# Issuing most of the V-cache transfers of a decode-attention kernel from ScalarE's queue

## The chip, the cores and the metric

The kernel runs on one core of one Trainium2 chip. The metric is the device time of one execution in microseconds (us); before the change it is 369.37 us, the median of three runs (369.34 to 369.59).

The core has five instruction streams that matter here: TensorE (PE, matrix products), VectorE (DVE), ScalarE (ACT), GpSimd (POOL) and SyncE (SP). A stream runs its instructions in order; a wait at the head of a stream holds everything behind it. Two of the streams, SP and ACT, issue the transfers between HBM and the on-chip memory in this kernel. The transfers themselves are carried by 16 DMA engines, which all streams share.

## The reference

One decode step with eight sequences (B = 8, one new token each, D = 576). Branch A is attention over the last W = 2048 positions of a cache; branch B is a small MLP; a gate per sequence mixes them.

```python
x = A_x; g = sigmoid((x * gate_w).sum(-1, keepdims=True))
# A: 32 query heads, 16 KV heads, Dh = 128, the last W = 2048 of 8192 positions
q = (x @ wq)                                  # per head 128 wide
k = repeat(k_cache[:, :, Sk - W:, :], 2)      # two query heads share a KV head
v = repeat(v_cache[:, :, Sk - W:, :], 2)
p = softmax(einsum("bhqd,bhkd->bhqk", q, k) * Dh ** -0.5)
a = einsum("bhqk,bhkd->bhqd", p, v) -> (B, 1, 32 * 128) @ wo
# B
b = gelu(layernorm(x) @ w1 + b1) @ w2 + b2
out = g * a + (1 - g) * b
```

All of it is bf16 in HBM. K and V in the window are 8 x 16 x 2048 x 128 elements each, 64 MiB each; the weights wq, wo, w1 and w2 add some 20 MB. The profile counts 154.31 MB read.

## The kernel before, in words

**Units.** K and V are each cut into 32 units of 2048 KB. A unit holds four sequences of one KV head, laid out as 128 rows of 16 KB, one row to a partition. Four units in a row (two KV heads, all eight sequences) form a group g; there are eight groups, and a softmax is done for each group at once.

**Slots.** The units, and the weights wo and w2, go through a ring of nine slots of on-chip memory (`NSLOT = 9`). Slots are handed out in the order of one list, `stream` (lines 549 to 560): K0 to K4, then K5, V0, K6, V1, K7, V2 and so on alternately, with a chunk of wo (W0 to W3, 1152 KB each, rows of 1152 bytes) after V7, V15, V23 and V31, then the bias b2 and four chunks of w2 (M0 to M3). The thing that takes a slot has to wait until the ninth thing before it in that list has been used up: a K unit's slot is free once VectorE has transposed it (`tr`, line 642, two per unit), a V unit's slot once TensorE has multiplied with it (`pv`, line 682).

**A K unit** (`k_unit`, line 624): its transfer (`dk`, line 627); two transposes on VectorE (line 642); two times eight matmuls of scores on TensorE (lines 659 and 173; `qk`). After the fourth K unit of a group comes the softmax (line 584): a maximum (`mx`, line 587), small operations, four exponentials on ScalarE (`exp`, line 601) and four transposes of the result on VectorE (line 606).

**A V unit** (`v_unit`, line 671): its transfer (`dv`, line 675), 16 matmuls (`pv`, line 682), a copy out of PSUM on ScalarE (`uev`, line 691, two buffers), four small matmuls (`us`, line 697), and for every second unit another small copy on ScalarE (`oev`, line 707) and a multiplication.

**The order.** No order is written out by hand. `_Plan.schedule` (line 62) lays out all operations with estimated costs: at each step it takes the ready operation with the earliest estimated start, each engine one after the other, all large transfers one after the other at an estimated bandwidth. Each engine then gets its operations in that order (`emit`, line 141) with waits on semaphores: one semaphore per engine, one per slot for the transfers (`"s%d" % s`). A V transfer is also kept behind the transfer before it in `stream` in the plan's time (`after=last_dma[-1:]`), which orders but adds no wait.

**Queues.** All 32 K, all 32 V, and all weight transfers are issued by SP, in the order of `stream`. ACT issues four small loads at the start (x, gate_w twice, b1) and one of the two output stores. PSUM and all compute stay as they are in the change.

Of the kernel before, what the change touches and what calls it, by code (L numbers as in the profile page):

```python
# [38 lines left out]
class _Plan:  # L39
# [10 lines left out]
    def add(self, eng, fn, deps=(), name=None, cost=0.1, after=(), prio=0):  # L50
        op = _Op(eng, fn, deps, name, cost, after=after, prio=prio)
        op.idx = len(self.all)
        self.all.append(op)
        return op

    def dma(self, eng, fn, semkey, nbytes, deps=(), name=None, after=(), prio=0):
        op = _Op(eng, fn, deps, name, self.DMA_ISSUE, after=after, is_dma=True, dma_sem=semkey, nbytes=nbytes, prio=prio)
        op.idx = len(self.all)
        self.all.append(op)
        return op  # L60
# [119 lines left out]
def build_kernel(nc, A_x, A_k_cache, A_v_cache, A_wq, A_wo, B_x, B_w1, B_b1, B_w2, B_b2, gate_w, out):  # L180
    B, Sq, D = A_x.shape
    _, Hkv, Sk, Dh = A_k_cache.shape
    Hq = A_wq.shape[1] // Dh
    F = B_w1.shape[1]
    W = min(4096, max(256, Sk // 4))
# [6 lines left out]
    NSLOT = 9  # L192
# [12 lines left out]
    with ExitStack() as es:  # L205
# [119 lines left out]
        def slot(s):  # L325
            return RAW[:, s * SE:(s + 1) * SE]
# [18 lines left out]
        OC = 64  # L345

        eng_sems = {e: es.enter_context(nc.semaphore("sem_" + e)) for e in ENGS}
        dma_keys = ["x", "b", "b2", "wq", "w1", "out", "outb"] + ["s%d" % i for i in range(NSLOT)] + ["t%d" % i for i in range(4)]
        dma_sems = {k: es.enter_context(nc.semaphore("dma_" + k)) for k in dma_keys}

        P = _Plan()
        add, dma = P.add, P.dma
# [39 lines left out]
        for s in range(2):  # L392
            o_xz.append(add("dve", (lambda s=s: lambda e: e.tensor_copy(xz[:, s, :].rearrange("p (k z) -> p k z", z=2)[:, :, s], x_sb[:, 512:576]))(),  # L393
                            deps=dx + [o_xz0], name="xz%d" % s, cost=0.12))
# [12 lines left out]
        for s in range(2):  # L407
            o_yz.append(add("dve", (lambda s=s: lambda e: e.tensor_copy(yz[:, s, :].rearrange("p (k z) -> p k z", z=2)[:, :, s], y_bf[:, 512:576]))(),
                            deps=[o_y, o_yz0], name="yz%d" % s, cost=0.12))
# [30 lines left out]
        def b1ev_fn(e):  # L440
# [5 lines left out]
                   deps=[o_dga, o_dgb, o_onesf], name="g_pe", cost=0.4, after=[o_yTp])  # L446
# [7 lines left out]
        for q in range(4):  # L454
            o_i32.append(add("dve", (lambda q=q: lambda e: e.tensor_copy(i32[32 * q:32 * q + 32, :], ident[32 * q:32 * q + 32, 32 * q:32 * q + 32]))(),
                             deps=[o_ident, o_obl], name="i32_%d" % q, cost=0.15, prio=-1))
# [91 lines left out]
        NUQ = 4 * NG  # L548
# [13 lines left out]
        last_dma = [d_w1r]  # L562
        slot_free = [[o_qp]] * 3 + [[o_hp]] * 3 + [[]] * 3
# [11 lines left out]
        def src_of(cache, g, q):  # L575
            hkv, b0 = 2 * g + q // 2, 4 * (q % 2)
            return cache[b0:b0 + 4, hkv, S0:Sk, :].rearrange("a (x r) d -> x a (r d)", x=32)

        def take_slot():
            n = n_slot[0]  # L580
            n_slot[0] += 1
            return (n + 6) % NSLOT
# [88 lines left out]
        def v_unit(i):  # L671
            g, q = divmod(i, 4)
            s = take_slot()
            item = 2 * g + q // 2
            d = dma("sp", lambda e: e.dma_start(slot(s), src_of(A_v_cache, g, q)), "s%d" % s, 4 * W * Dh * 2, deps=slot_free[s], name="dv%d" % i, after=last_dma[-1:])  # L675
            last_dma.append(d)

            def pv_fn(e):
                mm = None
                for t in range(16):  # L680
                    c = 32 * (t % 4)
                    mm = e.matmul(ps[c:c + 32, BK_OS[i % 2], :], PT[:, g % 2, 512 * q + 32 * t:512 * q + 32 * t + 32], slot(s)[:, 512 * t:512 * t + 512],  # L682
                                  start=(t < 4), stop=(t >= 12), skip_group_check=True, tile_position=(0, c))
                return mm
            deps = [d] + pt_done[g] + ([u_ev[i - 2]] if i >= 2 else [o_qT, o_u])
            prev = add("pe", pv_fn, deps=deps, name="pv%d" % i, cost=1.5, after=pv_hist[-1:])
            pv_hist.append(prev)
            slot_free[s] = [prev]
            if q == 3:
                pv_last[g] = prev  # L690
            u_ev[i] = add("act", lambda e: e.activation(out=EV[:, i % 2, :], in_=ps[:, BK_OS[i % 2], :], func=ACTF.Copy),  # L691
                          deps=[prev] + ([u_sum[i - 2]] if i >= 2 else []), name="uev%d" % i, cost=0.8, prio=3)

            def us_fn(e):
                mm = None
                for r in range(4):
                    mm = e.matmul(ps[:, BK_S, OC + 16 * (item % 2) + 8 * (q % 2):OC + 16 * (item % 2) + 8 * (q % 2) + 8], EV[:, i % 2, 128 * r:128 * r + 128], i32[:, 8 * r:8 * r + 8],  # L697
                                  start=(r == 0), stop=(r == 3), skip_group_check=True)
                return mm
            u_sum[i] = add("pe", us_fn, deps=[u_ev[i]] + o_i32 + b6_r[-2:], after=b6_w[-1:], name="us%d" % i, cost=1.0, prio=3)  # L700
            b6_w.append(u_sum[i])
            if q % 2 == 1:
                hl = q // 2
                prev = u_sum[i]
                osrc = ps[:, BK_S, OC + 16 * (item % 2):OC + 16 * (item % 2) + 16]
                if item < Hkv - 1:
                    ev = add("act", lambda e: e.activation(out=o32[:, item % 2, :], in_=osrc, func=ACTF.Copy), deps=[prev] + ([oT_done[item - 2]] if item >= 2 else []), name="oev%d" % item, cost=0.25, prio=3)  # L707
                    o_item_ev[item] = ev
                    b6_r.append(ev)
                    eng, src_, deps = "pool", o32[:, item % 2, :], [ev, rg_done[g]]  # L710
                else:
                    eng, src_, deps = "dve", osrc, [prev, rg_done[g]]

                def om_fn(e):
                    return e.tensor_tensor(out=oT[:, item, :, :].rearrange("p h b -> p b h"), in0=src_.rearrange("p (b h) -> p b h", h=2),  # L715
                                           in1=rg[:, g % 2, 16 * hl:16 * hl + 16].rearrange("p (b h) -> p b h", h=2), op=ALU.mult)
                oT_done[item] = add(eng, om_fn, deps=deps, name="oT%d" % item, cost=0.25, prio=9)
# [37 lines left out]
        for kind, i in stream:  # L755
            {"K": k_unit, "V": v_unit, "W": wo_chunk, "M": m2_chunk, "B": bias}[kind](i)
# [37 lines left out]
def bass_gated_mix__sliding_block_cached__mixer_channel_mlp__decode_kernel(  # L794
    nc: bass.Bass,
    A_x: bass.AP,
    A_k_cache: bass.AP,
    A_v_cache: bass.AP,
    A_wq: bass.AP,
    A_wo: bass.AP,  # L800
    B_x: bass.AP,
    B_w1: bass.AP,
    B_b1: bass.AP,
    B_w2: bass.AP,
    B_b2: bass.AP,
    gate_w: bass.AP,
    out: bass.AP,
):
    build_kernel(nc, A_x, A_k_cache, A_v_cache, A_wq, A_wo, B_x, B_w1, B_b1, B_w2, B_b2, gate_w, out)
# [28 lines left out]
```

## Time and profile before

| What | Value |
|---|---|
| median of three runs | 369.37 us |
| span of the profiled execution, first to last instruction | 367.9 us |
| its own whole time | not given apart from its span; the median lies 1.5 us above the span |
| TensorE busy | 263.5 us (72%), mean granted clock 0.852 of full |
| VectorE busy | 210.4 us (57%) |
| ScalarE busy | 47.8 us (13%) |
| queue of SP (q1) | 154.29 MB, its packets took 98.9% of the 16 DMA engines' span |
| queue of ACT (q10) | 56 packets, 0.03 MB |
| a V transfer, from issue to landing | 34.1 us median, 16.2 to 39.8 |
| a K transfer, from issue to landing | 33.3 us median, 20.1 to 40.5 |

How to read it: the time of a stream is "busy" only while it computes; waiting and issuing transfers don't count. The row of queues says how much of the time of all 16 DMA engines the packets of one queue filled. "From issue to landing" is the time a transfer spends waiting in its queue behind earlier ones and being carried; where it is many times what the carrying takes, there is a queue of transfers in front of it.

### The profile page before, as it was taken

Reading aid. Unit: us, or ns where it says so; the run is one execution under the profiler, and the core shown is the slowest. Engines: PE = TensorE matmul, PEld = TensorE weight load, DVE = VectorE, ACT = ScalarE, POOL = GpSimd, SP = SyncE. Lnnn points to the kernel's source line nnn. Section 1 sums busy time; section 2 is a strip of 40 time slices with the busy share of each in tenths; the row PEclk is TensorE's granted clock in tenths of the full one; section 3 lists DMA queues with packets and bytes.
Section 4 is the critical chain, followed back from the end, with each engine's and each line's share of the span. In section 5 each row is a group of like instructions: output and inputs, shape, how many; then the busy total and the mean of one; then the engine's idle time right before and its main releaser. Section 6 shows DMA issues by size and latency. Waiting matters only on the chain.

```text
span 367.9 us, 4129 instructions
## 1 busy us (share of the span) xinstructions
PE 263.5 (72%) x1837; PEld 87.0 (24%) x1429; DVE 210.4 (57%) x253; ACT 47.8 (13%) x117; POOL 37.5 (10%) x163
## 2 busy tenths in 40 slices
PE   0349984797698589773986399774976398773984
PEld 0339200122132022110321032110321032113542
DVE  0704599699686665459654674469544775364000
ACT  1010000210300220003000310003100300003200
POOL 7020011012011002000101002010110000000000
PEclk9999999699599869887897869886996879886659
DMA  8999999999999999999999999999999999999994
GB/s 345 428 412 424 435 430 433 428 428 428 433 429 431 422 433 426 428 435 427 433 431 433 408 434 432 429 426 433 433 436 428 414 434 424 431 433 440 402 429 193
DMA packets 14923, 154.59 MB, mean 420 GB/s; under 512 B 1292, under 2 KB 5428, under 8 KB 6072
## 3 DMA queue, kind: packets, MB, share of 16 engines
q1 hardware_dynamic: 14848, 154.29, 98.9%
q8 instruction: 13, 0.21, 0.2%
q10 hardware_dynamic: 56, 0.03, 0.0%
q14 instruction: 6, 0.05, 0.0%
HBM read 154.31 MB, written 0.01 MB: 419 GB/s over the span
## 4 chain that ended last, share of the span: by engine, by line
DMA 61%; PE 20%; DVE 16%; SPq 1%; issue 1%; ACT 0%; DVEq 0%; ACTq 0%
DMA arena<-in_A_k_cache_dram 50%; DMA arena<-in_B_w_dram 11%; DVE arena L642 10%; PE ps L173 9%; PE ps L659 3%; DVE arena L587 3%; PE ps L498 2%; PE ps L682 2%; PE ps L697 2%; DVE arena L606 1%; DVE arena L590 1%; PE ps L500 1%; SPq L675 1%; DVE arena L596 0%; SPq L746 0%
## 5 line engine op out<-in xcount | busy, mean ns | idle before, releaser
L642 DVE STREAM_TRANSPOSE arena<-arena 128x2048 f32<-128x2048 f32 x64 | 145.5, 2299 | 71.1 <-DMA arena<-in_A_k_cache_dram 60.1
L173 PE MATMUL ps<-arena 128*128 128x512 bf16 x408 | 141.3, 462 | 0.0
L659 PE MATMUL ps<-arena 128*128 128x512 bf16 x128 | 58.8, 459 | 21.4 <-DVE arena L642 21.3
L691 ACT ACTIVATE arena<-ps 128x512 f32<-128x512 f32 x32 | 19.1, 598 | 196.8 <-PE ps L682 196.8
L659 PEld LDWEIGHTS ps<-arena 128*128 128x128 bf16 x128 | 15.0, 117 | 124.6 <-issue 71.3
L635 POOL COPY arena<-arena 32x32 bf16<-32x32 bf16 x128 | 26.0, 203 | 159.8 <-PE ps L173 145.2
L697 PE MATMUL ps<-arena 128*128 128x8 f32 x256 | 35.3, 269 | 8.7 <-ACT arena L691 7.7
L697 PEld LDWEIGHTS ps<-arena 128*128 128x128 f32 x256 | 34.0, 208 | 21.8 <-ACT arena L691 15.2
L682 PE MATMUL ps<-arena 128*32 128x512 bf16 x512 | 36.4, 410 | 2.9 <-DMA arena<-in_A_v_cache_dram 2.9
L651 PE MATMUL ps<-arena 128*128 128x512 bf16 x8 | 4.7, 585 | 40.8 <-DVE arena L606 40.8
L587 DVE TENSOR_REDUCE arena<-ps 128x1 f32<-128x2048 f32 x8 | 18.3, 2282 | 21.6 <-PE ps L173 21.6
L601 ACT ACTIVATE arena<-ps,arena 128x512 bf16<-128x512 f32 x32 | 21.6, 686 | 40.9 <-DVE arena L596 40.9
L606 DVE STREAM_TRANSPOSE arena<-arena 128x512 bf16<-128x512 bf16 x32 | 19.9, 674 | 0.9 <-ACT arena L601 0.9
L682 PEld LDWEIGHTS ps<-arena 128*32 128x32 bf16 x512 | 11.3, 100 | 37.4 <-issue 27.1
L715 POOL TENSOR_TENSOR arena<-arena 128x16 bf16<-128x16 f32 x15 | 4.0, 266 | 141.7 <-ACT arena L707 141.7
L498 PE MATMUL ps<-arena 128*128 128x8 bf16 x144 | 10.9, 201 | 4.7 <-DMA arena<-in_B_w_dram 4.7
L541 PE MATMUL ps<-arena 128*8 128x288 bf16 (+1 forms) x140 | 11.9, 316 | 2.9 <-DMA arena<-in_B_w_dram 2.8
L498 PEld LDWEIGHTS ps<-arena 128*128 128x128 bf16 x144 | 10.8, 157 | 5.2 <-DMA arena<-in_B_w_dram 5.2
L651 PEld LDWEIGHTS ps<-arena 128*128 128x128 bf16 x8 | 0.9, 107 | 45.1 <-DVE arena L606 45.1
L613 DVE RECIPROCAL arena<-ps 128x32 f32<-128x32 f32 x8 | 2.9, 358 | 13.9 <-PE ps L611 13.9
L420 PE MATMUL ps<-arena 8*128 8x8 bf16 x8 | 0.5, 167 | 13.4 <-DVE arena L393 9.7
L715 DVE TENSOR_TENSOR arena<-ps,arena 128x16 bf16<-128x16 f32 x1 | 0.2, 229 | 16.7 <-PE ps L697 16.7
(83 smaller groups left out, 97.1 us busy)
## 6 DMA issues: line engine op xcount, KB each, us to landing
arena<-in_A_k_cache_dram SPq DMA_DIRECT2D x32, 2048.0 KB, 33.3
arena<-in_A_v_cache_dram SPq DMA_DIRECT2D x32, 2048.0 KB, 34.1
arena<-in_B_w_dram SPq DMA_DIRECT2D x1, 4608.0 KB, 24.3
arena<-in_A_wo_dram SPq DMA_DIRECT2D x4, 1152.0 KB, 36.6
arena<-in_A_wq_dram SPq DMA_DIRECT2D x1, 4096.0 KB, 13.0
arena<-in_B_w_dram SPq DMA_DIRECT2D x3, 1296.0 KB, 14.8
arena<-in_B_w_dram SPq DMA_DIRECT2D x2, 576.0 KB, 20.6
arena<-in_A_wq_dram SPq DMA_DIRECT2D x1, 512.0 KB, 3.6
```

The lines of the kernel that those rows point to most:

```text
L173: return e.add_instruction(mybir.InstMatmult(name=nc.get_next_instruction_name(), engine=mybir.EngineType.PE, ins=[e.lower_ap(rhs), e.lowe ...
L498: ins = e.matmul(out_, lhsT, yT[:, kt, :], start=(kt == 0), stop=False)
L541: ins = e.matmul(ps[32 * j:32 * j + 8, BK_ACC, 0:JN], lhsT, rhs[:, JN * j:JN * j + JN], start=False, stop=True, skip_group_check=True, til ...
L587: mx = add("dve", lambda e: e.tensor_reduce(out=k(MX), in_=ps[:, 0:4, :].rearrange("p a n -> p (a n)"), axis=AXL.X, op=ALU.max), deps=[qk_ ...
L601: return e.activation(out=Pm[:, 512 * c:512 * c + 512], in_=ps[:, c, :], func=ACTF.Exp, bias=k(NB), scale=SCALE, accum_out=k(SUM + c))
L606: pts.append(add("dve", (lambda c=c: lambda e: e.transpose(bass.AP(arena, offset=aoffs("PT") + 2048 * (g % 2) + 128 * c, ap=[[AST, 128], [ ...
L635: return e.tensor_copy(dst, src)
L642: tr = add("dve", (lambda h=h, kb=kb: lambda e: e.transpose(bass.AP(arena_f, offset=foffs("KT") + kb * 2048, ap=[[AST // 2, 128], [1, 2048]]),
L659: mm = e.matmul(*args, start=False, stop=last) if rc == 0 else held_matmul(nc, e, *args, stop=last)
L682: mm = e.matmul(ps[c:c + 32, BK_OS[i % 2], :], PT[:, g % 2, 512 * q + 32 * t:512 * q + 32 * t + 32], slot(s)[:, 512 * t:512 * t + 512], st ...
L691: u_ev[i] = add("act", lambda e: e.activation(out=EV[:, i % 2, :], in_=ps[:, BK_OS[i % 2], :], func=ACTF.Copy), deps=[prev] + ([u_sum[i - ...
L697: mm = e.matmul(ps[:, BK_S, OC + 16 * (item % 2) + 8 * (q % 2):OC + 16 * (item % 2) + 8 * (q % 2) + 8], EV[:, i % 2, 128 * r:128 * r + 128 ...
```

## The change

The first 26 of the 32 V transfers (V0 to V25) are issued by ACT and no longer by SP; V26 to V31, all K, wo, b2 and w2 stay on SP. The moved transfers count on nine semaphores of their own (`a0` to `a8`, one per slot), since a slot's K transfers still count on `s0` to `s8`.

```diff
-        dma_keys = ["x", "b", "b2", "wq", "w1", "out", "outb"] + ["s%d" % i for i in range(NSLOT)] + ["t%d" % i for i in range(4)]
+        dma_keys = ["x", "b", "b2", "wq", "w1", "out", "outb"] + ["s%d" % i for i in range(NSLOT)] + ["a%d" % i for i in range(NSLOT)] + ["t%d" % i for i in range(4)]
...
-            d = dma("sp", lambda e: e.dma_start(slot(s), src_of(A_v_cache, g, q)), "s%d" % s, 4 * W * Dh * 2, deps=slot_free[s], name="dv%d" % i, after=last_dma[-1:])
+            ring = "act" if i < NUQ - 6 else "sp"
+            d = dma(ring, lambda e: e.dma_start(slot(s), src_of(A_v_cache, g, q)), ("a%d" if ring == "act" else "s%d") % s, 4 * W * Dh * 2, deps=slot_free[s], name="dv%d" % i, after=last_dma[-1:])
```

`NUQ` is 32. In the program built from it, PE, DVE and POOL have the same instructions in the same order as before. ACT has 26 more transfer instructions with their waits, placed by the plan between its own operations, for instance (V transfers named `dv`):

```
q4_ev, dv0, dv1, uh, th, dv2, dv3, exp of group 0, uev0, dv4, dv5, uev1, oev0, dv6, uev2,
exp of group 1, uev3, dv7, oev1, uev4, dv8, uev5, dv9, oev2, uev6, dv10, exp of group 2, ...
```

SP's list is what remains: four weight loads, K0 to K12, W0, K13 to K20, W1, K21 to K28, W2, K29 to K31, V26 to V31, W3, b2, w2, one output store.

## The prediction

> **What bounds the kernel now.** I read the page's queue table and slices first, then the table by stages, then the chain of waits at the end, then SP's timeline, then what ACT waits for. From the page:
>
> ```profile
> span 367.9 us, 4129 instructions
> PE 263.5 (72%) x1837; PEld 87.0 (24%) x1429; DVE 210.4 (57%) x253; ACT 47.8 (13%) x117; POOL 37.5 (10%) x163
> DMA  8999999999999999999999999999999999999994
> q1 hardware_dynamic: 14848, 154.29, 98.9%
> q8 instruction: 13, 0.21, 0.2%
> q10 hardware_dynamic: 56, 0.03, 0.0%
> DMA 61%; PE 20%; DVE 16%; SPq 1%; issue 1%; ACT 0%; DVEq 0%; ACTq 0%
> arena<-in_A_v_cache_dram SPq DMA_DIRECT2D x32, 2048.0 KB, 34.1
> ```
>
> SP's queue alone fills 98.9% of the 16 DMA engines. The stage from V0's issue on (columns: length; busy time of PE, PEld, DVE, ACT, POOL; clock; DMA share; GB/s), and the end:
>
> ```profile
> 38.70:300.00 261.30, 194.79 (x1090) 47.25 (x727) 176.96 (x195) 36.06 (x92) 25.65 (x123) 0.84 1.01 429
> 350.00:365.00 15.00, 11.46 (x112) 5.83 (x104) 0.23 (x1) 0.60 (x1) 0.00 (x0) 0.74 0.88 366
> ```
>
> The engines have no gap where the change acts: share 1.01 at 429 GB/s. A K or V transfer is 2048 KB, 2.097 MB, so 4.9 us of all engines; each engine carries 8 of its 128 rows, 0.61 us a row. Issue to landing is 34.1 us, so about seven transfers are always issued ahead. PE (75% busy in the stage) and DVE (68%) follow the data. The end, from the chain and PE's timeline:
>
> ```profile
> 348.46 16.55 DMA arena<-in_B_w_dram
> 365.06 0.43 PE ps L541 x4
> ...
> 358.83 1.27 PE L541 MATMUL ps<-arena 128*8 128x288 bf16 x18 [0.40 <-DMA arena<-in_B_w_dram]
> 361.93 2.01 PE L541 MATMUL ps<-arena 128*8 128x288 bf16 x26 [1.82 <-DMA arena<-in_B_w_dram]
> 364.34 0.54 PE L541 MATMUL ps<-arena 128*8 128x288 bf16 x6 [0.41 <-DMA arena<-in_B_w_dram]
> 365.06 0.41 PE L541 MATMUL ps<-arena 128*8 128x288 bf16 x4 [0.18 <-DMA arena<-in_B_w_dram]
> ```
>
> The last w2 transfer is issued 16.55 us before it lands, behind others, so compute could free that slot some 14 us later without a gap on the engines. PE's own slack at the end is smaller: 0.40 + 1.82 + 0.41 + 0.18 = 2.8 us. SP around the first wo chunk, ACT's largest wait, and the first small loads:
>
> ```profile
> 95.74 0.59 SPq L723 DMA_DIRECT2D arena<-in_A_wo_dram  x1
> 107.98 18.53 SPq L627 DMA_DIRECT2D arena<-in_A_k_cache_dram  x1
> 126.56 0.82 SPq L675 DMA_DIRECT2D arena<-in_A_v_cache_dram  x1
> ...
> ACT arena L691 <- PE ps L682: 196.8, 30, 10.0
> ...
> 9.14 0.29 DVE L393 COPY arena<-arena 8x64 bf16<-8x64 bf16 x2 [9.14 <-DMA arena<-in_gate_w_dram]
> ```
>
> Behind each wo chunk the next issue (K13) is stuck for about 20 us (18.53 here, 22.29 at 184.43, 21.89 at 265.99); the seven transfers ahead cover it.
>
> **The change part by part.**
>
> *Bytes and rows:* the same transfers, the same 154.3 MB. If a row of 16 KB still takes 0.61 us, the engines need the same time, and nothing else can shorten it: cost 0.
>
> *Issuing:* SP loses 26 issues, ACT gains them, at 0.53 to 0.60 us each: 26 x 0.55 = 14.3 us on ACT, which is busy 47.8 us of 367.9 and waits 196.8 us for PV alone. Hidden by that idle time; uncovered (all 26 ahead of an exponential or copy that PE waits for) it would delay compute by at most 0.6 us at a time, and the seven transfers ahead cover that. The nine semaphores cost nothing: each wait only names another.
>
> *The wait moved:* SP waited for slots (129.4 us on transposes in 24 waits, the longest 11.6). ACT now stands in such waits with `uev`, `oev` and `exp` queued behind. PE's `us` waits for `uev`, PE's next `pv` but one for its buffer, DVE's transposes of line 606 for `exp`. Bounds: 0, where ACT arrives after the slot is free, and 11.6 us once. Nearest is the low end, since the V's stand among ACT operations of about the age of the work that frees their slots; 11.6 us of lateness is still under the 34 us issued ahead. Cost 0.
>
> *The order of arrival:* this is what changes. In one queue V0 lands after K5. In two, the engines take turns: at the start ACT's small loads, issued from 0.80 us, landed at 9.14 us while SP's 4 MB load, issued at 1.24, needed until 14.3. Neither queue was served to its end first, and a few KB took 8 us. So V0, issued at 38.7, shares with K1 to K5 and comes before K5; K's then come one in 9.8 us, the pace at which they came between V's already, but without their lead of five. Whoever comes too early waits in its slot, its queue runs empty, and the other has all the engines. A queue that is not empty is enough to keep them busy. Cost 0 as long as fewer than seven transfers' worth (34 us) is lost at once.
>
> *wo against V:* a wo chunk is 1152 KB in 1152-byte rows, 64 to an engine. If turns go row for row, W0 passes one short row per V row, 64 x 0.61 = 39 us if V's queue held that much; it holds at most four or five (20 to 25 us), then runs empty. So K13, K21 and K29 come later, by 0 (no turns lost) to 25 us, and then bunched at 4.9 us. I take 15 us, between them. The engines carry V meanwhile. DVE and PE recover: idle 32% and 25% of the stage, 0.25 us per us.
> The Trainium skill ("DMA: Bandwidth & Descriptors", section "Queues, rings and completion order") says that an engine drains a whole packet of typically 9 to 17 descriptors before it switches ring. By that rule wo would lose about 4 to 7 turns of a V transfer's size at most, much like the bound above; both readings leave the time at 0. The 9.14 us landing shows turns, not their size.
>
> *The end:* every K, V0 to V25 and W0 to W2 still precede V26 on the engines, so K31 lands when it did (VectorE's row for it starts at 320.50). K29 to K31 may come within 9.8 us instead of 20. PE then does three units of 16 score matmuls, 3.7 us warm (0.23 each) or 6.9 cold (0.43), and PV and `us` of 2.1: from 313 to 330.4 warm, 340 cold, against 328.3. Lateness 2 to 12 us; warm is nearer, since PE without a gap (43.6 to 58.5 us) ran at 0.23. 2 us is within the slack of 2.8: cost 0, upper bound 12 - 2.8 = 9.2 us.
>
> *The price of a turn:* no row shows two full queues. Low bound: in the first 10 us (2:12 in the queue table) ACT's 26 packets and SP's shared the engines at 426 GB/s, as before: 0. High bound: the instruction queue's 13 packets of 16 KB took 0.2% of 16 x 367.9 us, 0.9 us each instead of 0.61: 0.3 us more. V's 26 x 8 = 208 rows per engine at 0.3 us: 62 us. A gain is not excluded: 2.6% at most, if the engines held the best slice's 440 GB/s over 261 us, 6.5 us. I take 0; ACT's own loads are the nearest row, going the same way to the same memory.
>
> **Sum:** 367.9 us span + 0 (+0.1 for ACT's issues ahead of compute at the end) + 1.5 us between span and median = **369.5 us**.
>
> **The rivals.**
>
> *R1, turns cost (slower).* Rows alternate between a K and a V array and each turn stretches a little. For: the instruction packets' 0.9 us. Against: the 426 GB/s above. A tenth of the high bound, 0.03 us on 208 rows, is 6.2 us: 375.7 us. It decides from 0.004 us a row (0.74 / 208).
>
> *R2, the end bunches (slower).* As above with PE partly cold: lateness 5 us less 2.8 is 2.2 us: 371.6 us. For: the clock of 0.84 and three K's in a row behind W2. Against: warm clock when there is no gap. It decides from 3.5 us of lateness of the last softmax.
>
> *R3, ACT is held by SP's stuck issue (slower).* If what holds K13 for 18.5 to 22.3 us is common to both queues, ACT sticks in its V issue at W0, W1 and W2 with `uev` and `exp` behind it. The first two are recovered (20 us at 0.25 in some 80 us); of the third, at 266 to 288, 10 us are recovered by 328, and 10 - 2.8 = 7.2 remain: 376.7 us. For: K13's row. Against: SP's stuck issue follows wo in its own queue, and nothing shows ACT's. From a stall of 13 us it decides.
> The Trainium skill (same page and section) says that SP and ACT each own a ring, not a descriptor generator of their own; by it R3 would be possible. No run here shows it yet.
>
> *R4, faster (other side).* Two queues let an engine begin a row of one while it finishes the other. At 432 instead of 429 GB/s over 261 us: 1.8 us, 367.7 us. Limit 6.5 us. For: the best slices hold 435 to 440. Against: share 1.01, no gap to fill. From 0.3% it decides.
>
> *R5, the change does not do what it says:* ACT reaches its V's so late that K simply runs ahead and V follows. Then the order shifts back and the time stays: within the forecast.
>
> **How the numbers follow.** 0.2% of 369.37 is 0.74 us, about what a measurement of this kernel can tell from no change. No change (with R5) 0.45, own range 368.7 to 370.1; R1 0.20, R2 0.12, R3 0.08; R4 0.15. Slower 0.40, faster 0.15. The range goes from 367.5 (R4 with a little more, some 0.05 left below) to 376.5 (R1 above its tenth and most of R3 left out, some 0.10).
>
> **What the profile would show.** V's issues on ACT's queue and q10 with 26 x 2.1 = 54.5 MB; DMA share 1.01 and 429 GB/s in 38.7 to 300; V0 landing near K2 or K3; longer DVE waits for K after each wo; last landing at 365.1. Wrong: below 428 or above 431 GB/s in that stage (R1, R4); an ACT issue of more than 5 us (R3); `mx` of the last group after 332 and PE without idle time in 355 to 365 (R2); any slice of DMA share under 0.95 before 350.

## The result and the profile after

The changed kernel takes 372.41 us, the median of six runs (369.98 to 374.41), beside 369.39 us for the kernel before in the same comparison (six runs, 369.34 to 369.59). The ratio is 1.0076, with an interval of 1.0061 to 1.0092: it is slower by 3.0 us, 0.76%. The single runs of the changed kernel spread much wider than those of the kernel before, and the profiled one is the longest of the six (374.41 us, span 372.7), so what is read from its trace adds up to 4.8 us, not to 3.0.

The page after, its lines in the order of the page (span; the DMA slices; the two queues with packets, MB and share; the chain by engines; the issues with the time to landing):

```profile
span 372.7 us, 4106 instructions
...
DMA  8999999999999999999999999999999999999990
...
q1 hardware_dynamic: 11104, 99.76, 63.3%
q10 hardware_dynamic: 3800, 54.56, 34.3%
...
DMA 60%; PE 25%; DVE 12%; issue 1%; ACT 1%; ACTq 0%; POOL 0%; SPq 0%; DVEq 0%
...
arena<-in_A_k_cache_dram SPq DMA_DIRECT2D x32, 2048.0 KB, 36.9
arena<-in_A_v_cache_dram ACTq DMA_DIRECT2D x26, 2048.0 KB, 15.9
```

The change did what it says: 54.56 MB went through ACT's queue. The DMA engines have no gap, as before; only the last slice falls from 4 to 0, since the kernel goes on for longer after its last transfer. In the chain, PE's share rises from 20 to 25%. The stage from V0's issue on, in the columns of the stage table (length; busy PE, PEld, DVE, ACT, POOL; clock; DMA share; GB/s):

```profile
38.70:300.00 261.30, 182.99 (x1037) 45.33 (x702) 165.88 (x175) 32.57 (x83) 25.22 (x121) 0.84 1.01 429
```

Share and bandwidth are those of before to the last digit, 1.01 and 429 GB/s. What differs is how much compute was done by 300 us: PE 183.0 us instead of 194.8, DVE 165.9 instead of 177.0. The same bytes came in, but 11 to 12 us of the work on them lay still ahead. The start of PE's tail before, on PE's timeline (start; length; line; what it waited for; the end of that tail stands in the prediction):

```profile
336.33 0.64 PE L611 MATMUL ps<-arena 128*128 128x32 f32 x2 [5.07 <-DVE arena L610]
```

and the tail after:

```profile
342.25 0.63 PE L611 MATMUL ps<-arena 128*128 128x32 f32 x2 [6.24 <-DVE arena L610]
343.43 3.55 PE L698 MATMUL ps<-arena 128*128 128x8 f32 x16 [0.54 <-DVE arena L613]
...
360.96 1.88 PE L698 MATMUL ps<-arena 128*128 128x8 f32 x8 [0.70 <-ACT arena L692]
362.77 7.51 PE L541 MATMUL ps<-arena 128*8 128x288 bf16 x92
```

Before, the last products of line 541 (the MLP with w2, and the last piece of the projection with wo) stopped four times for w2 (0.40 + 1.82 + 0.41 + 0.18 us) and so ended with the transfers. After, they run through in one piece of 7.51 us and end at 370.3, while the last w2 landed at 364.9 (before 365.0). PE has become the bound of the tail.

**Where the lateness comes from.** The landing of a transfer is the moment at which its semaphore was raised for the last time, counted from the start of the span. In us:

| | K3 | V0 | K5 | K8 | K12 | K13 | K20 | K21 | K27 | K28 | W2 | K29 | K30 | K31 | last w2 |
|---|---|---|---|---|---|---|---|---|---|---|---|---|---|---|---|
| before | 47.5 | 62.0 | 57.1 | 86.3 | 125.2 | 137.9 | 206.0 | 219.2 | 278.0 | 287.8 | 295.7 | 300.5 | 310.2 | 320.5 | 365.0 |
| after | 51.6 | 53.1 | 71.0 | 97.1 | 136.0 | 154.8 | 218.7 | 233.3 | 291.9 | 301.6 | 305.8 | 310.7 | 315.5 | 320.3 | 364.9 |

V0 comes 9 us earlier and K5 14 us later; from there on every K up to K28 is 10 to 17 us behind its old place, and only K31 is back in it. The first wo chunk lies between K12 and K13, so the lead was lost before any wo. Nor is it that SP issued its K's too late: from issue to landing a K took 20.3 us at least and 36.9 in the median (33.3 before), so there were always K's in its queue. DVE's timeline of the kernel before, the transposes of K27, the maximum of group 6, the transposes of K31 and the last maximum:

```profile
278.05 4.50 DVE L642 STREAM_TRANSPOSE arena<-arena 128x2048 f32<-128x2048 f32 x2 [5.18 <-DMA arena<-in_A_k_cache_dram]
286.84 2.29 DVE L587 TENSOR_REDUCE arena<-ps 128x1 f32<-128x2048 f32 x1 [4.29 <-PE ps L173]
...
320.50 4.50 DVE L642 STREAM_TRANSPOSE arena<-arena 128x2048 f32<-128x2048 f32 x2 [5.75 <-DMA arena<-in_A_k_cache_dram]
328.30 2.29 DVE L587 TENSOR_REDUCE arena<-ps 128x1 f32<-128x2048 f32 x1 [3.29 <-PE ps L173]
```

The same of the kernel after:

```profile
291.92 4.51 DVE L642 STREAM_TRANSPOSE arena<-arena 128x2048 f32<-128x2048 f32 x2 [6.27 <-DMA arena<-in_A_k_cache_dram]
299.71 2.29 DVE L587 TENSOR_REDUCE arena<-ps 128x1 f32<-128x2048 f32 x1 [3.29 <-PE ps L173]
...
326.12 4.51 DVE L642 STREAM_TRANSPOSE arena<-arena 128x2048 f32<-128x2048 f32 x2 [1.85 <-PE ps L173]
334.21 2.29 DVE L587 TENSOR_REDUCE arena<-ps 128x1 f32<-128x2048 f32 x1 [3.59 <-PE ps L173]
```

and PE's first score product of K28 in it:

```profile
306.77 0.58 PE L651 MATMUL ps<-arena 128*128 128x512 bf16 x1 [6.12 <-DVE arena L606]
```

K27 is the last K of group 6. It lands 13.9 us late, the maximum of group 6 starts 12.9 us late, and PE can start K28's scores only when softmax 6 has read the scores of its own group, at 306.8. (PE stood for 6.12 us. The row names the transposes of line 606, but these last until 308.4; by the code this product depends on the four exponentials of line 601, and ScalarE's last one ends at 306.5.) From there PE has four units of scores with three PV's and the small products between them, 27.4 us in which it waits for nothing but two copies of 0.70 us. K31 landed at 320.5 before and at 320.3 after, but now DVE's transposes of it wait for PE and start at 326.1. So the last maximum follows that of group 6 by 34.5 us, all of it compute; before it followed by 41.5 us, because PE waited for K29 to K31. 12.9 us of lateness less the 7.0 us of waiting that is used up give the 5.9 us by which the last maximum is late (334.21 - 328.30).

**The sum in the profiled runs.** PE's tail starts 5.92 us later (342.25 - 336.33). The 2.81 us of waiting for w2 are gone. The work of the tail, from its first product to PE's end, takes 28.0 us (342.25 to 370.28) against 29.1 less 2.8, 26.3 us: 1.7 more. 5.9 - 2.8 + 1.7 = 4.8 us, the difference of the spans. The 1.7 us go with the clock: the same sixteen products of 128x8 took 1.95 us at 344.30 before and 3.58 at 350.44 after. Up to line 541 the tail lost 2.7 us so, and in line 541 it won 1.0 back. The rows of 340 to 360 of the stage table, before:

```profile
340.00:350.00 10.00, 9.30 (x81) 6.16 (x85) 0.00 (x0) 2.16 (x5) 0.54 (x2) 0.67 1.01 411
350.00:360.00 10.00, 8.89 (x80) 4.65 (x72) 0.23 (x1) 0.60 (x1) 0.00 (x0) 0.62 1.02 429
```

and after:

```profile
340.00:350.00 10.00, 7.21 (x50) 5.07 (x50) 2.71 (x7) 2.40 (x7) 0.27 (x1) 0.50 1.01 414
350.00:360.00 10.00, 9.29 (x64) 6.17 (x56) 0.00 (x0) 1.38 (x3) 0.27 (x1) 0.50 1.02 423
```

The granted clock (the third figure from the end) is 0.50 in both rows after, 0.67 and 0.62 before.

### The profile page after: what moved, and what is told of

It reads as the page before. It is cut to its first block, busy times and chain, and to the rows that moved or that the text cites. A ratio compares the mean times of both kernels' runs of the same rounds, so it can differ in the third digit from the quotient of the medians.

```text
span 372.7 us, 4106 instructions
## 1 busy us (share of the span) xinstructions
PE 255.8 (69%) x1815; PEld 88.1 (24%) x1429; DVE 210.2 (56%) x253; ACT 47.7 (13%) x117; POOL 37.7 (10%) x163
## 3 DMA queue, kind: packets, MB, share of 16 engines
q10 hardware_dynamic: 3800, 54.56, 34.3%
## 4 chain that ended last, share of the span: by engine, by line
DMA 60%; PE 25%; DVE 12%; issue 1%; ACT 1%; ACTq 0%; POOL 0%; SPq 0%; DVEq 0%
DMA arena<-in_A_k_cache_dram 58%; PE ps L173 10%; DVE arena L642 7%; PE ps L698 4%; PE ps L683 4%; PE ps L659 3%; DMA arena<-in_B_b_dram 3%; PE ps L541 2%; DVE arena L587 2%; DVE arena L606 1%; PE ps L464 1%; ACT arena L692 1%; DVE arena L596 0%; DVE arena L590 0%; PE ps L651 0%
## 5 line engine op out<-in xcount | busy, mean ns | idle before, releaser
L173 PE MATMUL ps<-arena 128*128 128x512 bf16 x401 | 136.3, 451 | 15.2 <-ACT arena L692 11.0
L659 PE MATMUL ps<-arena 128*128 128x512 bf16 x115 | 52.1, 453 | 21.5 <-DVE arena L642 21.3
L698 PE MATMUL ps<-arena 128*128 128x8 f32 x256 | 36.9, 275 | 8.7 <-ACT arena L692 7.7
L698 PEld LDWEIGHTS ps<-arena 128*128 128x128 f32 x256 | 35.6, 217 | 22.4 <-ACT arena L692 16.4
L651 PE MATMUL ps<-arena 128*128 128x512 bf16 x6 | 3.5, 586 | 42.7 <-DVE arena L606 42.7
L587 DVE TENSOR_REDUCE arena<-ps 128x1 f32<-128x2048 f32 x8 | 18.3, 2282 | 16.4 <-PE ps L173 16.4
L683 PEld LDWEIGHTS ps<-arena 128*32 128x32 bf16 x512 | 11.5, 100 | 33.5 <-issue 26.7
L498 PE MATMUL ps<-arena 128*128 128x8 bf16 x144 | 10.9, 201 | 4.6 <-DMA arena<-in_B_w_dram 4.6
L541 PE MATMUL ps<-arena 128*8 128x288 bf16 (+1 forms) x140 | 10.9, 314 | 0.0
## 6 DMA issues: line engine op xcount, KB each, us to landing
arena<-in_A_k_cache_dram SPq DMA_DIRECT2D x32, 2048.0 KB, 36.9
```

The lines of the kernel that those rows point to most:

```text
L173: return e.add_instruction(mybir.InstMatmult(name=nc.get_next_instruction_name(), engine=mybir.EngineType.PE, ins=[e.lower_ap(rhs), e.lowe ...
L498: ins = e.matmul(out_, lhsT, yT[:, kt, :], start=(kt == 0), stop=False)
L541: ins = e.matmul(ps[32 * j:32 * j + 8, BK_ACC, 0:JN], lhsT, rhs[:, JN * j:JN * j + JN], start=False, stop=True, skip_group_check=True, til ...
L587: mx = add("dve", lambda e: e.tensor_reduce(out=k(MX), in_=ps[:, 0:4, :].rearrange("p a n -> p (a n)"), axis=AXL.X, op=ALU.max), deps=[qk_ ...
L659: mm = e.matmul(*args, start=False, stop=last) if rc == 0 else held_matmul(nc, e, *args, stop=last)
```

## The experiments

The theory: the transfers are neither slower nor dearer; K loses its lead over V, the last softmaxes come late, PE's tail has some 2.8 us of slack, and the rest is the loss. Rivals: ACT's transfer issues delay ACT's own work; or the halved clock in the tail makes the loss, and lateness matters only through it. Later the theory itself split: is it the bunching of K29 to K31 (the prediction's R2), or the late softmax 6?

**1. Four V's fewer on ACT.**

```diff
-            ring = "act" if i < NUQ - 6 else "sp"
+            ring = "act" if i < NUQ - 10 else "sp"
```

> Only V0 to V21 on ACT, V22 to V31 on SP; PE, DVE and POOL keep their order. Lost lead (my theory: V in a queue of its own overtakes K, K28 to K30 land 13.7, 10.1 and 5.3 us late, the last softmax starts 5.9 us late, and PE cannot hide it): from K28 on everything goes through one queue again, K29 lands near 301 us instead of 311, the last maximum starts at 328 to 329 us instead of 334.2, time 369.2 to 369.8 us. ACT's line (the cost is ACT's extra issues and waits): 22 of 26 issues stay, so about 22/26 of the 3.0 us, 371.9 us. Turns of wo against V: wo after V7 and V15 keep their turns, the third does not: 371 us or so.

Measured: 369.59 us (369.44 to 370.08), ratio 1.0003 (0.9994 to 1.0012): no loss. The first K's are as late as in the changed kernel (K5 at 70.7, K13 at 154.0), but ACT's queue runs out with V21 at 266.5, K25 to K27 then follow each other at 4.8 us, and K27 lands at 278.0. The maximum of group 6 starts at 289.67, the last one at 327.89, and PE waits for w2 again:

```profile
364.87 0.41 PE L541 MATMUL ps<-arena 128*8 128x288 bf16 x4 [0.16 <-DMA arena<-in_B_w_dram]
```

Twenty-two transfer issues among ACT's operations, then, cost nothing; and lateness that is made good before the last two groups costs nothing either.

**2. All 32 V's on ACT.**

```diff
-            ring = "act" if i < NUQ - 6 else "sp"
+            ring = "act"
```

> All 32 V on ACT, order of PE, DVE and POOL unchanged. Lost lead: V26 and V27 also overtake K30 and K31, so K31 lands later than 320.9 us, by up to two transfers (4.9 to 9.8 us), the last maximum starts 3 to 8 us later than in the changed kernel, time 375 to 381 us. ACT's line: six more issues, at 3.0 us for 26 that is 0.7 us more: 373.1 us.

Measured: 381.48 us, the median of three runs (381.19 to 383.60; a fourth took 388.60 and isn't in the ratio), ratio 1.034 (1.0317 to 1.0363). K29 to K31 now take turns with V26 to V28, and K31 lands at 337.0, 16.6 us later than in the changed kernel and not 4.9 to 9.8. The last maximum starts at 344.78, 10.6 us later and not 3 to 8. The loss has the direction and somewhat more than the size expected. Here it is K31 itself that sets it, and not softmax 6: the maximum of group 6 starts at 297.28, earlier than in the changed kernel, and PE waits 2.79 us for the transposes of K31.

**3. The order alone.** All transfers stay on SP; the list `stream` is written out in the order in which they landed in the changed kernel.

```diff
-        stream = [("K", i) for i in range(5)]
...
+        seen = """K0 K1 K2 K3 V0 K4 V1 K5 V2 K6 V3 K7 V4 K8 V5 K9 V6 K10 V7 K11 V8 K12 V9 V10 W0
...
+          K29 K30 K31 V26 V27 V28 V29 V30 V31 W3"""
+        stream = [(n[0], int(n[1:])) for n in seen.split()]
```

> One queue (SP) as before, but the list of transfers is put in the order in which they landed in the changed kernel: V0 after K3, V9 and V10 ahead of the first wo chunk, K29 to K31 in a row behind the third; slots and plan follow that list. Lost lead: the order alone does the harm, last maximum after 332 us, time 371 to 375 us. ACT's line or anything that belongs to two queues: nothing on ACT, no turns, so 369.4 us as before.

Measured: 369.56 us median (369.34 to 372.75), ratio 1.003 (1.0008 to 1.0052). The expectation missed for the median: seven of twelve runs lie at 369.3 to 369.6, five at 372.0 to 372.8. In the profiled run, one of the seven, K27 landed at 288.0, 4 us before its landing in the changed kernel, the maximum of group 6 started at 294.60 and the last one at 328.02. The list also moved the plan's order on PE. So this kernel stands at the edge, with a smaller lateness than it was meant to copy, and shows only that one queue can lose the time too.

**4. PE kept busy through the last softmax.** In the changed kernel, 34 matmuls of 128x384 whose result is used by nothing are put on PE between the last score products and the last row sum (in the trace they stand ahead of the two PV's there, at 332.90, and last 5.70 us).

```diff
+        N_WARM = 34
...
+                    for _ in range(N_WARM):
+                        mm = e.matmul(ps[:, BK_S, 128:512], ident, maskR[:, 0:384], start=True, stop=True, skip_group_check=True)
...
+                warm = add("pe", warm_fn, deps=[qk_unit[4 * g + 3]] + b6_r[-2:], after=[qk_unit[4 * g + 3]] + pv_hist[-1:], name="warm", cost=6.0, prio=2)
```

> The changed kernel with 34 extra matmuls (128x384, into unused columns of PSUM bank 6) on PE behind the last score matmuls, where PE otherwise idles 6.2 us before the last row sum. They are meant to keep PE's clock up. The landings and the last softmax stay late (334 us). If the tail after it is long because PE runs at a granted clock of 0.50 there (19.4 us from 343.4 to 362.8), it becomes 11 to 14 us and the time falls to 369.4 to 370.5 us. If the clock is not what counts, or PE's small matmuls do not keep it up, the time stays at 372 to 374 us.

Measured: 370.31 us (369.4 to 371.88), ratio 1.0024 (1.0009 to 1.0039), 0.8 us above the kernel before. The last maximum is late as in the changed kernel (332.88; 334.21 and, in experiment 7, 332.81 there), but the clock of the tail's beginning is not halved:

```profile
340.00:350.00 10.00, 8.99 (x76) 6.60 (x66) 1.37 (x5) 2.26 (x5) 0.27 (x1) 0.73 1.01 411
```

With 0.73 instead of 0.50 in that stretch, some 2 of the 3 us are gone; the tail takes 26.8 us (340.91 to 367.73) in the profiled run. The clock after PE's pause is thus a part of the loss, and of the lateness's price.

**5. Lateness alone, at the last maximum.** In the kernel before, one, two or three idle transposes of 2.3 us are put on VectorE ahead of the last maximum; all transfers stay as they are. (The diff is that for one; N_LATE is 2 and 3 in the others.)

```diff
+        N_LATE = 1
...
+            hold = []
+            for _ in range(N_LATE if g == NG - 1 else 0):
+                hold.append(add("dve", lambda e: e.transpose(bass.AP(arena_f, offset=foffs("KT"), ap=[[AST // 2, 128], [1, 2048]]),
...
+                                deps=[qk_unit[4 * g + 3]] + hold[-1:], name="hold", cost=0.0, prio=5))
```

> The kernel before with one idle VectorE transpose (2.3 us, on buffers no longer needed) between the last score matmul and the last maximum; nothing else moved. The last softmax is 2.3 us late with all transfers where they were. PE's idle time at the end is 2.8 us, so the time should stay within 0.3 us of 369.4. If there is no slack it is 371.7 us.

> The kernel before with two idle transposes of 2.3 us ahead of the last maximum (they add work and change no result). If the lateness of the last softmax less a slack of 2.8 us is the loss, 4.6 us late cost 1.8 us: 371.3. If instead the lateness costs more because PE's clock is halved in the tail, 372 to 373. If the slack were as large as the slots' (14 us): 369.5.

> The same with three such transposes: the last softmax 6.9 us late, a little more than the 5.9 us of the changed kernel, with all transfers where they were. If the lateness of the last softmax is the whole cause, this kernel loses at least as much as the changed one: 6.9 - 2.8 = 4.1 us at an unchanged clock, 373.5 us, and up to 375 us when PE's clock falls in the longer pause. If something else of two queues costs the time, it is under 371 us.

| idle transposes | added work | time (range) | above before | ratio (interval) | time of the profiled run | last maximum in it | PE's tail in it |
|---|---|---|---|---|---|---|---|
| 1 | 2.3 us | 369.59 (369.43 to 371.67) | 0.0 | 1.0008 (0.9998 to 1.0018) | 371.67 | 330.20 | 338.24 to 367.54, 29.3 us |
| 2 | 4.6 us | 372.90 (369.89 to 374.44) | 3.4 | 1.0076 (1.0048 to 1.0104) | 372.80 | 331.31 | 339.35 to 368.67, 29.3 us |
| 3 | 6.9 us | 374.04 (370.27 to 375.52) | 4.5 | 1.0106 (1.0064 to 1.0147) | 375.27 | 335.00 | 343.04 to 371.04, 28.0 us |

With three transposes, the last maximum and the start of PE's tail:

```profile
335.00 2.29 DVE L593 TENSOR_REDUCE arena<-ps 128x1 f32<-128x2048 f32 x1
```

```profile
343.04 0.64 PE L617 MATMUL ps<-arena 128*128 128x32 f32 x2 [12.03 <-DVE arena L616]
```

Lateness of the last softmax with every transfer in its old place makes the loss: 4.6 us of added work cost 3.4 us and 6.9 us cost 4.5. One transpose is covered in nine of eleven runs; the other two, the profiled one among them, lie at 371.6. The maximum itself came 1.9, 3.0 and 6.7 us after the 328.30 of the kernel before; with two transposes it is less late than the work added, since the scores ended 1.7 us earlier in that run (326.62). A fixed slack of 2.8 us would have given 1.8 and 4.1 by the added work, so for two transposes the theory with the clock in it (372 to 373) fits and the bare slack does not. The last column says why: in these tails the clock was 0.50 and they took 28.0 to 29.3 us, not 26.3. The kernel before begins its own tail at 336.33; 29.3 us from there end at 365.6, and the last w2 lands at 365.0. With a clock of 0.50 it has hardly any slack (experiment 1's tail, at 0.50 from 335.92, waited for w2 0.42 + 0.16 us), and with the warmer tail that its profile shows it has 2.8.

**6. wo in ACT's queue.** The changed kernel with W0 to W2 issued by ACT as well.

```diff
-            d = dma("sp", lambda e: e.dma_start(dst[:, :, 0:D], A_wo[128 * h0:128 * (h0 + WO_CH), :].rearrange("(t p) c -> p t c", p=128)),
-                    "s%d" % s, WO_CH * 128 * D * 2, deps=slot_free[s], name="d_wo%d" % i, after=last_dma[-1:])
+            d = dma("act" if i < 3 else "sp", lambda e: e.dma_start(dst[:, :, 0:D], A_wo[128 * h0:128 * (h0 + WO_CH), :].rearrange("(t p) c -> p t c", p=128)),
+                    ("a%d" if i < 3 else "s%d") % s, WO_CH * 128 * D * 2, deps=slot_free[s], name="d_wo%d" % i, after=last_dma[-1:])
```

> The changed kernel with the first three wo chunks on ACT's queue too, in line behind V7, V15 and V23, so K never waits behind wo. Lost lead: K is late from the first V on, by 10 us before any wo, so the last maximum stays at 332 us or later, 371 to 374 us. Turns of wo: K28 to K30 come early again, 369.4 to 370.3 us. If the issue behind a wo chunk sticks for about 20 us on ACT as it does on SP, ACT's copies and exponentials stand behind it, and the time is above 375 us.

Measured: 383.02 us (381.55 to 383.41), ratio 1.0358 (1.0343 to 1.0373). From ACT's timeline, the V issue behind W1, and from ACT's waits, the copies behind such issues (total, times, longest):

```profile
195.87 23.90 ACTq L676 DMA_DIRECT2D arena<-in_A_v_cache_dram  x1
```

```profile
ACT arena L692 <- issue: 31.3, 2, 23.4
```

The issue that gets stuck stands behind wo in the queue that wo is in: on ACT 23.90 us behind W1 and 8.44 behind W2 (0.71, not stuck, behind W0), while SP's issues of K13 to K31 took 0.53 to 0.54. On ACT it holds PV's copies for up to 23.4 us. In the changed kernel, with wo on SP, ACT's 26 issues took 0.54 us in the middle and 0.82 at most, while SP's issues behind the three chunks took 12.6 to 17.2.

The K's came early again, as the second expectation had it: K13 lands at 135.5, before its old place, K27 at 281.1, 3.1 us late instead of 13.9, and K31 at 308.4. So the queue that carries wo is the one that falls behind, and the lateness of K27 in the changed kernel needs both: the lost lead, and wo in K's own queue, without which the lead comes back. The time is still longer, and the stuck issue is not what the end waits for. W2, behind V23 on ACT, lands only at 324.9, and PE, which works in order, stands before the piece of the projection that needs it, ahead of the rest of the scores:

```profile
324.97 2.08 PE L541 MATMUL ps<-arena 128*8 128x288 bf16 x16 [11.19 <-DMA arena<-in_A_wo_dram]
```

The maximum of group 6 had started at 296.61, earlier than in the changed kernel; the last one starts at 344.75. What the time would be with K early and W2 in time, this run doesn't show.

**7. The changed kernel once more.**

> The changed kernel once more, to see what its spread of 370.0 to 374.4 us comes from. Transfers land as in the first profile; if PE's clock at the end makes the spread, a faster execution shows the same landings and last maximum within 1 us, but a higher granted clock in 340 to 362.

Measured: 372.88 us (370.31 to 374.05), ratio 1.0078 (1.0048 to 1.0108). In its profile (373.10 us) the transfers land nearly as in the first profile (K27 291.5, K31 320.1), the maximum of group 6 starts at 298.13, the last one at 332.81, and the tail, at 0.50 again in 340 to 360, ends at 369.0. The last softmax thus moves by 1.4 us between two runs of the same kernel, with the clock of that stretch the same, and the two times lie 1.3 us apart. Between these two it was the softmax, and not the clock, that made the difference; what makes the whole spread isn't shown.

**8. Two V's fewer on ACT.**

```diff
-            ring = "act" if i < NUQ - 6 else "sp"
+            ring = "act" if i < NUQ - 8 else "sp"
```

> V0 to V23 on ACT, V24 to V31 on SP (two fewer than in the change). My theory now: the K transfers are late by 10 to 14 us from the first V's on, K27 still lands near 290, so the softmax of group 6 is still late and K28's scores start behind it; with the four score units and PV on PE after that, the last maximum starts at 331 to 334 and the time is 370.5 to 372. Rival, only the bunch K29 to K31 matters: with V24 and V25 back in SP's queue between these K's, they are spread again, K29 lands about where it did before (301 to 305), the last maximum starts before 330, and the time is 369.5.

Measured: 369.74 us (369.38 to 372.23), ratio 1.0024 (1.0008 to 1.004). K27 landed at 287.8 and K29 at 300.8, where it lands before the change; the maximum of group 6 started at 295.28 and the last one at 329.26. By its numbers this goes to the rival's side, though not by its reason: the last maximum follows that of group 6 by 34.0 us, as in the changed kernel (34.5 and 34.7 there), with no wait of PE for a K. K27 came 2 us earlier than the 290 expected (4 us earlier than in the changed kernel), and that put the last maximum at the edge.

**9. Softmax 6 late, all transfers early.** The kernel before, with five idle transposes ahead of the maximum of group 6.

```diff
+        N_LATE = 5
...
+            for _ in range(N_LATE if g == NG - 2 else 0):
```

> The kernel before, all transfers on SP, with five idle transposes of 2.3 us ahead of the maximum of group 6 (the last but one; they add work and change no result). Only softmax 6 is delayed, by 11.5 us, to a start of its maximum near 298.3; every K lands as early as before. My theory: the last maximum comes 34.5 us after that of group 6 (PE has four score units, PV and the small products between them, without a gap), so at 332 to 333.5, and the time is 372 to 373.5 as with the change. Rival, the bunch of K29 to K31 is needed: with these K's spread as before, PE works them off as they land, the last maximum starts before 330, and the time is 369.5.

Measured: 375.89 us (372.24 to 377.8), ratio 1.0151 (1.0104 to 1.0198). DVE's timeline:

```profile
284.59 11.70 DVE L590 STREAM_TRANSPOSE arena<-arena 128x2048 f32<-128x2048 f32 x5 [2.07 <-PE ps L173]
296.32 2.29 DVE L593 TENSOR_REDUCE arena<-ps 128x1 f32<-128x2048 f32 x1
...
334.18 2.29 DVE L593 TENSOR_REDUCE arena<-ps 128x1 f32<-128x2048 f32 x1 [3.58 <-PE ps L173]
```

The last maximum starts where it does in the changed kernel (334.18 and 334.21), though K28 to K31 come one by one between V's. So the bunch isn't needed; a late softmax 6 is enough. The distance between the two maxima was 37.9 us, more than the 34.5 expected: the plan had put a row sum and small products ahead of K28's scores, which so began only at 310.0, 13.7 us after the start of the maximum (7.1 in the changed kernel). The time is 2.4 us above the range expected (the profiled run, 376.12, 2.6 above). The last maximum is 0.7 us above its own range; PE's tail took 29.3 us (342.21 to 371.53) instead of the 28.0 of the changed kernel, 1.3 more; and the time lies 2.2 us above the span here, 1.7 there.

## Why the prediction was right or wrong

The likeliest case, no change at 369.5 us, was wrong by 2.9 us. The rival R2, a late end, came, at 371.6 forecast and 372.4 measured. That its number is so near is in part luck. R2 had 5 us of lateness from the bunch of K29 to K31 with PE partly cold; the runs show 5.9 us from a late softmax 6, with the scores at full clock (1.00 in 320 to 330), and a tail that costs more than the formula has.

- *Bytes, rows, price of a turn:* right. The stage holds 429 GB/s and a share of 1.01; the median packet of 16 KB takes 611 ns with two full queues as with one. R1 and R4 fall by this.
- *Issuing, and the wait moved:* right. 22 or 26 V issues on ACT showed no cost (experiment 1; issues of 0.54 us).
- *Order of arrival:* the order was right (V0 next to K3, then one K in 9.7 us), and that K loses its lead of five. Its price was wrong: the lead was weighed only against the seven transfers issued ahead, that is, by whether the DMA engines run dry. It had a second use: it let the softmax of group 6 end early, so that PE met K28 to K31 as they landed. Lost lead isn't a backlog that idle time works off: the data itself comes later, so idle time before it arrives is of no use. PE and DVE didn't recover a share of it on the way; the 12.9 us stood until K27.
- *wo against V:* K13, K21 and K29 came 16.9, 14.2 and 10.1 us late, near the 15 us taken, but the lost lead alone had made K12 10.9, K20 12.7 and K28 13.8 us late; wo's own part is +6.0, +1.5 and -3.7 us. The 15 us were thus near for a reason that the sum didn't have in it. Of its two readings of a turn, row for row is the one that the trace shows. Between 138 and 142 us, with W0 in SP's queue and V9 and V10 in ACT's (packets, MB, share):

```profile
q10 hardware_dynamic: 111, 1.57, 92.2%
q1 hardware_dynamic: 111, 0.13, 8.8%
```

1.57 MB are 96 rows of 16 KB (the other 15 packets have under 512 bytes), 0.13 MB are 111 short rows: about one short row for one row of V. V10 landed at 145.3 and V11 was issued only at 146.0; with V's queue empty the rest of W0 passed at once (1.26 MB in SP's queue between 144 and 147), and W0 landed at 147.5, 11.5 us behind K12. In the kernel before it landed 3.0 us behind V7, the transfer ahead of it. The 9 to 17 descriptors that the Trainium skill gives for a turn ("DMA: Bandwidth & Descriptors", section "Queues, rings and completion order") are not what this trace shows, if a row is one descriptor.

- *The end:* this is the step that failed. It had K29 to K31 bunched (right: 310.7, 315.5, 320.3), PE beginning three units at 313, and 2 us of lateness. But PE stood four units from the end, not three: K28's scores couldn't begin before softmax 6 had read its own, at 306.8, and K29's began at 317.7. The three units from there took 16.4 us, somewhat less than the 17.4 of the sum. The lateness was 5.9 us. The view that was not read was the one above: what the last softmax but one waits for, and how far it lies ahead of the last.
- *The slack of 2.8 us* was that of one execution with a tail at 0.62 to 0.67. Experiment 5 shows that 2.3 us of added work are covered in most runs, and that beyond it the price is that of a tail at 0.50. R2's formula, lateness less slack, lacked this term: 1.7 us in the profiled runs.
- *R3* falls by ACT's issues of at most 0.82 us in the changed kernel; experiment 6 shows its mechanism where wo is in ACT's queue, but not its price, since the end there waited for W2. By the Trainium skill's sentence on descriptor generators ("DMA: Bandwidth & Descriptors", section "Queues, rings and completion order") the stall could have been common to both queues; here it followed wo's queue.
- *What the profile would show* held: 54.56 MB on q10, 429 GB/s, V0 near K3, the last w2 at 364.9, the DMA slices up to 350 as before (the first, from 0 to 9 us, is under 0.95 in both kernels and says nothing); and of R2's signs, the last maximum after 332 and PE in 355 to 365 without a wait for w2.

## What to carry to other kernels

A queue that is issued in order also fixes the order of arrival; a second queue replaces it by taking turns, whatever the bandwidth does. Before splitting a queue, ask which of its transfers run ahead of their partners and what that lead is for at the end of the kernel: read the landing of the last few inputs of each softmax (or other serial step), not only whether the engines stay full. And price lateness against the tail with the clock that a pause leaves behind, for the slack in one profile may belong to a warmer run.

## What the runs showed of the hardware

- Two full queues share the DMA engines at no cost: 611 ns a row and 429 GB/s, as with one. With rows of 16 KB in both, they go about one for one (from K3 on one K and one V in 9.7 us). With rows of 1152 bytes in one of them it is again about one for one (111 short rows beside 96 of 16 KB in 138 to 142 us), so the queue with the short rows nearly stands still until the other runs empty.
- An issue behind a transfer of 1152 KB in 1152-byte rows can be stuck (18.5 to 22.3 us on SP before, 12.6 to 17.2 on SP after; 23.9, 8.4 and, behind W0, 0.7 on ACT in experiment 6) in the queue of that transfer alone; the other queue's issues go through in 0.54 us meanwhile.
- After PE's pause of 6 us in the last softmax, the granted clock stayed at 0.50 from 340 to 360 us although PE was busy 93% of 350 to 360 with small products. The tail takes 28.0 to 29.4 us so, and 26.3 without its waits for w2 in the profile of the kernel before, whose clock was 0.67 and 0.62 in these rows. What decides when it comes back isn't shown. The runs' own mean clocks go along with a part in the loss: with two idle transposes, the three runs at 369.9 to 370.1 us have a mean clock of 0.852, the seven at 372.8 to 374.4 one of 0.835 to 0.844. That the clock makes that difference is argued from this, and from experiment 4, not shown by itself; in experiment 7 two runs differ by 1.3 us at the same clock in the tail.
